# Another conversion of the float64 weights in the first feed-forward layer and in the weight maker, on other steps of the program

## The chip, the cores and the metric

The kernel runs on one core of one Trainium2 chip. The metric is the time of one execution on the device, in microseconds (us). The engines are named as the profile names them: PE (TensorE, matrix products), PEld (its weight loads), DVE (VectorE), ACT (ScalarE), POOL (GpSimd) and SP (SyncE, which here only issues transfers).

## The reference

Three layers follow each other: a causal linear attention with a decaying state per head ("retention"), and two feed-forward layers without a gate. The second and third read float64 weights, the rest is float32.

```python
# 4 batches, 8 heads, 768 positions, 64 wide
state = gamma * state + k[t] outer v[t];  y[t] = scale * q[t] @ state
x = y as (3072 tokens, 512)
h = x @ w_in          # 512 x 2048, float64
x = (h * sigmoid(1.702 * h)) @ w_out     # 2048 x 512, float64
h = x @ moe2_w_in;  r = maximum(h, 0)
out = (r * r) @ moe2_w_out
```

## The kernel before

**Retention.** 24 units of 128 tokens are worked through in the loop of line 553, one step `u` per unit, and one step more. On PE a step is `scores(u)` (L449) and then `outputs(u - 1)`: the products with the masked scores (L498), the update of the state (L508) and the product with the old state (L519). Every sixth unit begins a batch and has no old state, every sixth ends one and has no update. DVE masks the scores (`pt`, L458) and scales the result (L532, L536, L539); ACT scales `v` by head (`vs`, L473; for the first six units POOL does it, L468) and copies the state (L515). A unit is 1 MB, loaded by SP in two halves (L440) into one of four buffers, three steps ahead of its use.

**Slices.** The first feed-forward layer's weights come as 32 slices of 128 x 512 float64 values (512 KB each), in the order of the list `order` (lines 96 to 102): for block `f` of 128 hidden units, slice `(f, 0)` is a part of `w_in` and `(f, 1)` a part of `w_out`. Each is turned into two float32 parts, a high one (the fp32r type that PE reads) and a low one, and PE multiplies low, high and high with (high, high, low) of the activations. `cv_load` issues the load of a slice on POOL's queue into one of three `raw` buffers, at most three slices ahead of the conversions. `cv_a` lets ACT scale the high words into `hm` (L129), at most two ahead. `cv_step` converts: on DVE five instructions on words that take the high part's bits (`top`) and what is left of the mantissa (L158, L156, L166, L173, L177) and one product that gives the low part (L180), on ACT the copy of the high part (L176).

In the retention `cv_step` is called in every step (line 560), and converts on those where its first argument isn't 0 and a scaled slice is there: steps 4, 5, 6, 8, 9, 10 and every second one up to 24, 13 slices in all. The scores' mask and the scaling of the result (`masked`, `scaled`) are put between its instructions.

**First feed-forward layer.** Four blocks `n` of 512 tokens go through 16 steps `f` each (line 707): `up(n, f)` is 12 matmuls with slice `(f, 0)`, and from the third step on `down(n, f - 2)` is 12 matmuls with slice `(f - 2, 1)`. Behind `up`, ACT applies the activation (`gs`, L589, one buffer), rounds it to the high part (`gh`, L590, two buffers), and DVE subtracts it for the low part (`gl`, L594). `down` reads `gh` and `gl`. In block `n = 0` each step also calls `cv_step` (L597), with `gl` put ahead of its last instruction, and a second time at f = 3, 6 and 9: the other 19 slices. In blocks 1 to 3 `background` takes pieces of the generator `make`, up to 4.8 (line 604) of the costs that the pieces give as they yield.

**The maker.** `make` forms, for the second half of the tokens of that layer and for the last layer, sums and differences of weight blocks (seven products in the place of eight), splits them in two parts and writes them to `kw` in DRAM: `make_first` from the slices, `make_second` from 32 more float64 slices that ACT's queue loads (L233), ACT scales (L295) and DVE converts (lines 322 to 340), each written by POOL's queue (L302). What is left by then runs in the stages behind, in portions of 1.8 (lines 815 and 828).

**Last stages.** From line 744 on four blocks of seven-product work run, each an `up2` and a `down2`. Their weights `r` are read from `kw` by SP (L703) as eight buffers come free; all products are of line 756. At its fifth step (`p == 4`) `up2` issues the loads of the next block's activations on POOL's queue (L628, four of 512 KB).

Of the kernel before, what the change touches and what calls it, by code (L numbers as in the profile page):

```python
# [13 lines left out]
U32 = mybir.dt.uint32  # L14
ACTF = mybir.ActivationFunctionType
# [3 lines left out]
P = 128  # L19
# [23 lines left out]
BG = 4.8  # L43
BGUP = 1.8
# [10 lines left out]
def tile_retention_then_two_ffns(  # L55
# [64 lines left out]

    def cv_a():


        n = cv["a"]
        if n == min(cv["load"], cv["b"] + 2):
            return
        cv["a"] += 1
        hm = cv_p.tile([P, 512], F32, tag="hm", name=f"hm{n}")
        nc.scalar.mul(hm, cvt[n][0][:, :, 1].bitcast(F32), 2.0 ** -112)  # L129
        cvt[n].append(hm)  # L130

    def cv_step(limit=len(order), f1=None, f2=None, load=True):

# [4 lines left out]
        if limit is None or n >= min(limit, ready):  # L138
            for f in (f1, f2):
                if f is not None:  # L140
                    f()
        else:
            cv["b"] += 1
            raw, hm = cvt.pop(n)
            hb = hm.bitcast(U32)
            low, high = raw[:, :, 0], raw[:, :, 1]
            f, half = order[n]
            w = wpool[f].tile([P, 4, 2, P], F32R, tag=f"w{half}", name=f"w{n}")
            ws[order[n]] = w
            if cv["pool"] is not None:  # L150
                top, rest = cv["pool"].tile([P, 512], U32, tag="top", name=f"top{n}", bufs=1), high
            else:
                top, rest = high, hb
# [4 lines left out]
            v.tensor_scalar(  # L158
                out=top, in0=hb, scalar1=3, scalar2=0x7FFFF000,
                op0=ALU.logical_shift_left, op1=ALU.bitwise_and,  # L160
            )
            if rest is high:
                do_rest()
            elif f1 is not None:
                f1()
            v.scalar_tensor_tensor(  # L166
                out=top, in0=hb, scalar=0x80000000, in1=top, op0=ALU.bitwise_and, op1=ALU.bitwise_or
            )
            if rest is hb:
                do_rest()  # L170
            elif f1 is not None:
                f1()
            v.scalar_tensor_tensor(  # L173
                out=low.bitcast(F32), in0=low, scalar=2.0 ** -32, in1=rest, op0=ALU.mult, op1=ALU.add
            )
# [4 lines left out]
            v.scalar_tensor_tensor(  # L180
                out=w[:, :, 1], in0=low.bitcast(F32).rearrange("p (k c) -> p k c", c=P), scalar=2.0 ** -20,
                in1=hm.rearrange("p (k c) -> p k c", c=P), op0=ALU.mult, op1=ALU.mult
            )
# [103 lines left out]
    def make_second():  # L287

        with tc.tile_pool(name="k2", bufs=2, side="right", reuse_waits="tile") as pool:
            hms = {}  # L290

            def scale(n):
                if n < len(jobs):
                    hm = pool.tile([P, 512], F32, tag="hm", name=f"hm2_{n}")
                    hms[n] = hm, later(lambda: nc.scalar.mul(hm, raws[n][:, :, 1].bitcast(F32), 2.0 ** -112))  # L295
# [16 lines left out]
            for n in range(len(jobs)):  # L312
                hm, done = hms.pop(n)
                while not done:
# [7 lines left out]
                v.tensor_scalar(  # L322
                    out=wu, in0=hb, scalar1=3, scalar2=0x7FFFFFFF,
                    op0=ALU.logical_shift_left, op1=ALU.bitwise_and,
                )
                yield 0.45
                v.scalar_tensor_tensor(
                    out=wu, in0=hb, scalar=0x80000000, in1=wu, op0=ALU.bitwise_and, op1=ALU.bitwise_or
                )
# [723 lines left out]
```

## Time and profile before

| | us |
|---|---|
| three timed runs | 1069.56, 1072.49, 1075.27 |
| their median | 1072.49 |
| span of the profiled execution | 1070.7 |
| PE busy in it | 1049.9 (98%) |
| DVE busy | 796.5 (74%) |
| ACT busy | 511.6 (48%) |
| POOL busy | 95.0 (9%) |
| mean granted clock of PE | 0.998 of full speed |

The profiled execution is told by its span, from the first to the last instruction; no separate time of it is given, and the span lies 1.8 us under the median of the timed runs. The page cuts the span in 40 slices and gives each engine's busy share in tenths: PE stands at 9 in all but the first two and the last one, while DVE's row moves between 3 and 9. The mean busy share of PE hides where its 20.8 idle us are, so it has to be read by stage. A busy PE is not yet a PE at its peak: matmuls are pipelined, so a step's length is read from the start of one group of matmuls to the start of the next.

### The profile page before, as it was taken

What the parts mean: (1) busy time and instruction counts of PE and PEld (TensorE: products, weight loads), DVE (VectorE), ACT (ScalarE), POOL (GpSimd) and SP (SyncE); (2) the same over time, 40 slices, a digit from 0 to 9 for tenths busy, and PEclk for the clock granted to TensorE, in tenths of its full rate; (3) what the DMA queues carried; (4) which work ended last, traced back from release to release, by engine and by line L of the source; (5) the groups of instructions that cost most, each with busy time, mean ns of one, the idle gap of its engine ahead of it and who ended that gap; (6) DMA issues with size and microseconds to landing.
All of it is one profiled execution on the core that took longest, in us unless ns stands there. A gap on an engine that the chain in (4) does not pass through costs nothing.

```text
span 1070.7 us, 15321 instructions
## 1 busy us (share of the span) xinstructions
PE 1049.9 (98%) x5482; PEld 870.7 (81%) x5482; DVE 796.5 (74%) x1197; ACT 511.6 (48%) x862; POOL 95.0 (9%) x143
## 2 busy tenths in 40 slices
PE   8799999999999999999999999999999999999998
PEld 6788888888888888887888887888888888888886
DVE  4988897888698889855598587889345887345953
ACT  5787554433454545454546343455233465233443
POOL 3100110111111121101000001000100000000000
PEclk9999999999999999999999999999999999999999
DMA  9997677855467685599866799766876667766664
GB/s 331 339 330 275 249 247 255 318 191 191 180 223 248 202 323 189 172 360 317 299 208 204 247 295 326 238 216 210 290 213 193 194 210 230 219 193 192 203 205 163
DMA packets 106652, 259.34 MB, mean 242 GB/s; under 512 B 11216, under 2 KB 11344, under 8 KB 106320
## 3 DMA queue, kind: packets, MB, share of 16 engines
q1 hardware_dynamic: 79088, 156.64, 45.2%
q0 software_dynamic: 22304, 83.89, 21.3%
q10 hardware_dynamic: 5184, 17.83, 5.3%
q8 instruction: 44, 0.72, 0.3%
q14 instruction: 32, 0.26, 0.1%
HBM read 184.91 MB, written 73.40 MB: 241 GB/s over the span
## 4 chain that ended last, share of the span: by engine, by line
PE 89%; DMA 6%; DVE 3%; ACT 1%; SPq 0%; issue 0%; POOL 0%; POOLq 0%; ACTq 0%
PE D L756 28%; PE X L756 15%; PE Z L756 7%; PE y L614 5%; PE h L583 5%; PE h L582 5%; PE y L613 5%; PE y L615 5%; PE h L584 5%; PE Y L756 4%; DMA r<-kw 3%; DMA unit<-qkv 3%; DVE pt L458 1%; PE sc L449 1%; PE yp L519 1%; DMA raw<-w 1%
## 5 line engine op out<-in xcount | busy, mean ns | idle before, releaser
L756 PE MATMUL D<-gx,r 128*128 128x512 f32 x1344 | 306.3, 389 | 0.0
L756 PEld LDWEIGHTS D<-gx,r 128*128 128x128 f32 x1344 | 252.0, 188 | 53.0 <-DVE gx L859 0.8
L859 DVE TENSOR_TENSOR gx<-g,gx 128x1024 fp32r<-128x1024 f32 x112 | 136.3, 1219 | 36.9 <-ACT gx L858 36.7
L858 ACT CAST gx<-g 128x1024 fp32r<-128x1024 f32 x112 | 116.6, 1051 | 93.0 <-PE D L756 83.4
L756 PE MATMUL X<-xh,r 128*128 128x512 f32 x512 | 157.9, 390 | 1.6 <-DMA r<-kw 1.6
L777 ACT COPY g<-X 128x512 f32<-128x512 f32 x96 | 56.4, 588 | 188.5 <-PE X L756 188.5
L782 DVE TENSOR_TENSOR g<-Z,g 128x512 f32<-128x512 f32 x64 | 44.2, 690 | 126.1 <-ACT g L777 93.6
L756 PEld LDWEIGHTS X<-xh,r 128*128 128x128 f32 x512 | 95.9, 188 | 22.6 <-issue 2.8
L582 PE MATMUL h<-hl,w 128*128 128x512 f32 x256 | 99.7, 389 | 0.0
L615 PE MATMUL y<-gl,w 128*128 128x512 f32 x256 | 99.6, 389 | 0.0
L756 PE MATMUL X<-xl,r 128*128 128x512 f32 x256 | 99.6, 389 | 0.0
L584 PE MATMUL h<-hl,w 128*128 128x512 f32 x256 | 99.6, 389 | 0.0
L614 PE MATMUL y<-gh,w 128*128 128x512 f32 x256 | 99.6, 389 | 0.0
L583 PE MATMUL h<-hl,w 128*128 128x512 f32 x256 | 99.6, 389 | 0.0
L613 PE MATMUL y<-gh,w 128*128 128x512 f32 x256 | 99.6, 389 | 0.0
L590 ACT CAST gh<-gs 128x512 fp32r<-128x512 f32 x64 | 39.8, 622 | 87.2 <-PE y L614 84.8
L756 PE MATMUL Z<-xh,r 128*128 128x512 f32 x256 | 79.3, 391 | 1.0 <-DMA r<-kw 0.9
L589 ACT ACTIVATE gs<-h 128x512 f32<-128x512 f32 x64 | 38.2, 597 | 64.5 <-PE h L584 51.6
L594 DVE TENSOR_TENSOR gl<-gs,gh 128x512 fp32r<-128x512 f32 x64 | 44.0, 688 | 32.0 <-ACT gh L590 32.0
L756 PEld LDWEIGHTS Z<-xh,r 128*128 128x128 f32 x256 | 47.7, 188 | 12.3 <-DMA r<-kw 2.3
L613 PEld LDWEIGHTS y<-gh,w 128*128 128x128 f32 x256 | 48.0, 188 | 10.1
L582 PEld LDWEIGHTS h<-hl,w 128*128 128x128 f32 x256 | 48.1, 188 | 10.0
(105 smaller groups left out, 1590.7 us busy)
## 6 DMA issues: line engine op xcount, KB each, us to landing
r<-kw SPq DMA_DIRECT2D x448, 256.0 KB, 2.9
kw<-wq POOLq DMA_DIRECT2D x32, 896.0 KB, 6.5
unit<-qkv SPq DMA_DIRECT2D x47, 512.0 KB, 7.5
raw<-w POOLq DMA_DIRECT2D x32, 512.0 KB, 6.0
kw<-wh POOLq DMA_DIRECT2D x16, 1024.0 KB, 4.7
kw<-w SPq DMA_DIRECT2D x16, 512.0 KB, 4.7
raw<-win ACTq DMA_DIRECT2D x16, 512.0 KB, 4.3
raw<-wout ACTq DMA_DIRECT2D x16, 512.0 KB, 4.7
```

The costliest lines, as they stand in the source:

```text
L582: nc.tensor.matmul(hp, lo[:, k], xh, start=(k == 0), stop=False)
L583: nc.tensor.matmul(hp, hi[:, k], xh, start=False, stop=False)
L584: nc.tensor.matmul(hp, hi[:, k], xl, start=False, stop=(k == KD - 1))
L594: v.tensor_tensor(out=gl, in0=g, in1=gh, op=ALU.subtract)
L613: nc.tensor.matmul(a, lo[:, e], gh, start=s0, stop=False)
L614: nc.tensor.matmul(a, hi[:, e], gh, start=False, stop=False)
L615: nc.tensor.matmul(a, hi[:, e], gl, start=False, stop=s1)
L756: nc.tensor.matmul(a, w, b, start=start, stop=stop, skip_group_check=True)
L777: nc.scalar.copy(out=t, in_=a)
L782: v.tensor_tensor(out=t, in0=a, in1=t, op=ALU.add)
L858: nc.scalar.copy(out=hi, in_=src)
L859: v.tensor_tensor(out=lo, in0=src, in1=hi, op=ALU.subtract)
```

## The change

The conversion of a slice has other instructions, and they stand in other steps.

- `scale_words`: ACT scales the high words into `hm` as before and, new, the low words by 2 to the -29 in place, as integers (3 bits are left of them).
- `join`: two DVE instructions put the 31 bits and the sign together from `hm`, over the high words' place.
- `round_up`: one DVE instruction adds the low word's 3 bits to the lower 16-bit half of the result (every second 16-bit value), with the sum kept from overflowing by a minimum.
- ACT copies the high part from that (L182 now), and the low part is now the difference of the whole and the copy. That instruction (L187) is put in a list, `tails`, and issued in the next `cv_step` behind its first instruction and `f1`. `hm` has three buffers.
- The conversions of the retention are called for on steps 4, 6, ... 22 (`CVU`), and the first loads at step 3. At step 4 no slice is scaled yet, so the conversions stand on steps 6 to 22, nine of them.
- In block `n = 0` each step calls `cv_step` twice until the slices are at an end, 23 of them by f = 11; behind that `background` begins.
- `make_second` uses the same parts: three DVE instructions where there were five, and one ACT instruction more.

```diff
+CVU = range(4, NU, 2)
+    def scale_words(hm, raw):
+        nc.scalar.mul(hm, raw[:, :, 1].bitcast(F32), 2.0 ** -112)
+        nc.scalar.mul(raw[:, :, 0], raw[:, :, 0], 2.0 ** -29)
+    def join(out, hb, other):
+        v.tensor_scalar(
+            out=other, in0=hb, scalar1=3, scalar2=0x7FFFFFFF,
+            op0=ALU.logical_shift_left, op1=ALU.bitwise_and,
+        )
+        yield
+        v.scalar_tensor_tensor(
+            out=out, in0=hb, scalar=0x80000000, in1=other, op0=ALU.bitwise_and, op1=ALU.bitwise_or
+        )
+        yield
+    def round_up(w, raw):
+        half = w.bitcast(U16).rearrange("p (c t) -> p c t", t=2)[:, :, 0]
+        v.scalar_tensor_tensor(out=half, in0=half, scalar=65527.0, in1=raw[:, :, 0], op0=ALU.min, op1=ALU.add)
...
-        hm = cv_p.tile([P, 512], F32, tag="hm", name=f"hm{n}")
-        nc.scalar.mul(hm, cvt[n][0][:, :, 1].bitcast(F32), 2.0 ** -112)
+        hm = cv_p.tile([P, 512], F32, tag="hm", name=f"hm{n}", bufs=3)
+        scale_words(hm, cvt[n][0])
...
-            def do_rest():
-                v.tensor_scalar(out=rest, in0=hb, scalar1=0x1FF, scalar2=None, op0=ALU.bitwise_and)
...
-            v.scalar_tensor_tensor(
-                out=low.bitcast(F32), in0=low, scalar=2.0 ** -32, in1=rest, op0=ALU.mult, op1=ALU.add
-            )
-            nc.scalar.copy(out=w[:, :, 0], in_=top.bitcast(F32).rearrange("p (k c) -> p k c", c=P))
-            v.tensor_scalar(out=hb, in0=top, scalar1=0xFF800000, scalar2=None, op0=ALU.bitwise_and)
+            steps = join(hm.bitcast(U32), hm.bitcast(U32), raw[:, :, 1])
+            next(steps)
+            if f1 is not None:
                 f1()
+            cv_tail()
+            next(steps)
+            round_up(hm, raw)
+            nc.scalar.copy(out=w[:, :, 0], in_=hm.rearrange("p (k c) -> p k c", c=P))
             if f2 is not None:
                 f2()
...
+            def tail():
+                v.tensor_tensor(
+                    out=w[:, :, 1], in0=hm.rearrange("p (k c) -> p k c", c=P), in1=w[:, :, 0], op=ALU.subtract
+                )
+                ws[key] = w
+            tails.append(tail)
...
-                v.tensor_scalar(out=hb, in0=wu, scalar1=0xFF800000, scalar2=None, op0=ALU.bitwise_and)
-                yield 0.45
-                v.scalar_tensor_tensor(
-                    out=hm, in0=raw[:, :, 0], scalar=2.0 ** -52, in1=hm, op0=ALU.mult, op1=ALU.mult
-                )
+                round_up(wf, raw)
...
-                v.tensor_tensor(out=wf, in0=wf, in1=hm, op=ALU.add)
-                yield 0.7
...
-                cv_step(2 * WA if u >= 3 and (u % 2 != 1 or u in (3, 5, 9)) else 0, masked, scaled, u >= 2)
+                cv_step(2 * WA if u in CVU else 0, masked, scaled, u >= 3)
...
-            if n == 0:
+            if n == 0 and cv["b"] < len(order):
                 cv_step(len(order), None, low)
-                if f in (3, 6, 9):
-                    cv_step()
+                cv_step()
```

Three places show it in the engines' order. The first is DVE in two steps of the retention's middle, before: every step's mask (`pt`) stands among a slice's six instructions.

```order
L158 TENSOR_SCALAR top_685<-hm_571 128x512
L156 TENSOR_SCALAR raw_476<-hm_571 128x512
L166 SCALAR_TENSOR_TENSOR top_685<-hm_571,top_685 128x512
L458 TENSOR_TENSOR pt_647<-sc_638,tab_sb 128x1024
L173 SCALAR_TENSOR_TENSOR raw_476<-raw_476 128x512
L177 TENSOR_SCALAR hm_571<-top_685 128x512
L532 TENSOR_TENSOR x_0_680<-yp_657,ytab_136 128x2x128
L532 TENSOR_TENSOR x_1_681<-yp_657,ytab_136 128x2x128
L180 SCALAR_TENSOR_TENSOR w_684<-raw_476,hm_571 128x4x128
L158 TENSOR_SCALAR top_746<-hm_682 128x512
```

And now, in the same engine and stage:

```order
L130 TENSOR_SCALAR raw_338<-hm_450 128x512
L461 TENSOR_TENSOR pt_562<-sc_553,tab_sb 128x1024
L135 SCALAR_TENSOR_TENSOR hm_450<-hm_450,raw_338 128x512
L143 SCALAR_TENSOR_TENSOR hm_450<-hm_450,raw_338 128x512
L535 TENSOR_TENSOR x_0_444<-yp_572,ytab_135 128x2x128
L535 TENSOR_TENSOR x_1_445<-yp_572,ytab_135 128x2x128
L461 TENSOR_TENSOR pt_617<-sc_608,tab_sb 128x1024
L535 TENSOR_TENSOR x_0_650<-yp_627,ytab_136 128x2x128
L535 TENSOR_TENSOR x_1_651<-yp_627,ytab_136 128x2x128
L187 TENSOR_TENSOR w_595<-hm_450,w_595 128x4x128
```

One instruction of a slice stands ahead of the mask in the place of three, the next step has none but the tail, and a slice takes two steps.

The second place is DVE at f = 1 of the first feed-forward layer's block 0, before: one slice.

```order
L158 TENSOR_SCALAR raw_1378<-hm_1492 128x512
L166 SCALAR_TENSOR_TENSOR raw_1378<-hm_1492,raw_1378 128x512
L156 TENSOR_SCALAR hm_1492<-hm_1492 128x512
L173 SCALAR_TENSOR_TENSOR raw_1378<-raw_1378,hm_1492 128x512
L177 TENSOR_SCALAR hm_1492<-raw_1378 128x512
L594 TENSOR_TENSOR gl_1_1511<-gs_1_1509,gh_1_1510 128x512
L180 SCALAR_TENSOR_TENSOR w_1514<-raw_1378,hm_1492 128x4x128
```

Now the same step on DVE, from its first slice to the next step's `gl`:

```order
L130 TENSOR_SCALAR raw_1321<-hm_1423 128x512
L187 TENSOR_TENSOR w_1428<-hm_1365,w_1428 128x4x128
L135 SCALAR_TENSOR_TENSOR hm_1423<-hm_1423,raw_1321 128x512
L143 SCALAR_TENSOR_TENSOR hm_1423<-hm_1423,raw_1321 128x512
L597 TENSOR_TENSOR gl_1_1454<-gs_1_1452,gh_1_1453 128x512
L130 TENSOR_SCALAR raw_1426<-hm_1434 128x512
L187 TENSOR_TENSOR w_1457<-hm_1423,w_1457 128x4x128
L135 SCALAR_TENSOR_TENSOR hm_1434<-hm_1434,raw_1426 128x512
L143 SCALAR_TENSOR_TENSOR hm_1434<-hm_1434,raw_1426 128x512
```

And on ACT there, where the second slice's copy and the scaling of the slice after next now stand between one `gh` and the next `gs`:

```order
L592 ACTIVATE gs_1_1452<-h_1_1439 128x512
L593 CAST gh_1_1453<-gs_1_1452 128x512
L182 CAST w_1457<-hm_1423 128x4x128
L125 ACTIVATE hm_1464<-raw_1437 128x512
L126 ACTIVATE raw_1437<-raw_1437 128x512
L182 CAST w_1469<-hm_1434 128x4x128
L125 ACTIVATE hm_1475<-raw_1467 128x512
L126 ACTIVATE raw_1467<-raw_1467 128x512
L592 ACTIVATE gs_2_1495<-h_2_1480 128x512
```

Where one slice's copy and one scaling stood between two activations there are now six instructions, and each tail (L187) reads what ACT has copied just before.

The third place is POOL's queue around the first `up2`'s loads of activations (`xb`), before: three of the maker's writes (`kw`) stand between the end of the first layer (`ykept_122`) and those loads, and more behind them.

```order
L623 DMA ykept_122<-y_1_4445 128x1024
L302 DMA kw_112<-wq_4374 128x7x256
L302 DMA kw_112<-wq_4599 128x7x256
L302 DMA kw_113<-wq_4726 128x7x256
L628 DMA xb_0_0_0_4810<-ykept_119 128x1024
L628 DMA xb_0_0_1_4811<-ykept_119 128x1024
L628 DMA xb_0_1_0_4814<-ykept_120 128x1024
L628 DMA xb_0_1_1_4815<-ykept_120 128x1024
L302 DMA kw_113<-wq_4851 128x7x256
L302 DMA kw_114<-wq_4979 128x7x256
```

Now the last of the maker's writes (`kw_116`) stands ahead of them:

```order
L625 DMA ykept_122<-y_1_4485 128x1024
L314 DMA kw_115<-wq_4409 128x7x256
L314 DMA kw_115<-wq_4565 128x7x256
L314 DMA kw_116<-wq_4688 128x7x256
L314 DMA kw_116<-wq_4769 128x7x256
L630 DMA xb_0_0_0_4844<-ykept_119 128x1024
L630 DMA xb_0_0_1_4845<-ykept_119 128x1024
```

The maker is at an end seven of its writes earlier, counted against the loads.

## Rows read from the trace of the kernel before

**Rows 1.** Busy us by stretch: stretch, length, busy (instructions) of each engine, clock, DMA share, GB/s.

```profile
0.00:104.00 104.00, 89.79 (x1257) 78.60 (x1258) 82.68 (x151) 77.30 (x248) 15.79 (x28) 0.98 0.91 328
104.00:453.00 349.00, 349.00 (x1543) 288.98 (x1542) 301.57 (x556) 166.34 (x255) 49.40 (x68) 1.00 0.65 228
453.00:528.00 75.00, 73.19 (x321) 59.47 (x320) 41.65 (x72) 37.91 (x65) 7.78 (x10) 1.00 0.92 328
607.00:683.00 76.00, 75.28 (x331) 61.74 (x330) 56.48 (x96) 29.92 (x48) 7.98 (x11) 1.00 0.89 296
```

**Rows 2.** PE by time, retention: start us, us, engine, line, operation [idle before].

```profile
38.31 1.16 PE L449 MATMUL sc<-unit 64*128 64x128 f32 x16
...
63.58 1.16 PE L449 MATMUL sc<-unit 64*128 64x128 f32 x16 [2.10 <-DMA unit<-qkv]
...
72.49 1.16 PE L449 MATMUL sc<-unit 64*128 64x128 f32 x16
...
76.16 1.16 PE L449 MATMUL sc<-unit 64*128 64x128 f32 x16
...
98.38 1.16 PE L449 MATMUL sc<-unit 64*128 64x128 f32 x16 [0.26 <-DMA unit<-qkv]
...
104.12 0.48 PE L582 MATMUL h<-hl,w 128*128 128x512 f32 x1
```

**Rows 3.** Waits of PE, 0 to 110 us: total, times, longest.

```profile
PE sc L449 <- DMA unit<-qkv: 5.7, 6, 2.1
PE yp L498 <- DVE pt L458: 4.2, 4, 2.5
```

**Rows 4.** DVE by time in one step of the retention.

```profile
45.20 0.41 DVE L158 TENSOR_SCALAR top<-hm 128x512 uint32<-128x512 uint32 x1
45.54 0.42 DVE L156 TENSOR_SCALAR raw<-hm 128x512 uint32<-128x512 uint32 x1
...
49.81 0.41 DVE L158 TENSOR_SCALAR top<-hm 128x512 uint32<-128x512 uint32 x1
```

**Rows 5.** Busy us by stretch, one microsecond of the retention (columns as in rows 1).

```profile
65.00:66.00 1.00, 1.00 (x12) 1.00 (x10) 1.00 (x2) 1.00 (x5) 0.00 (x0) 0.50 1.02 422
```

**Rows 6.** ACT by time, block 0 of the first feed-forward layer.

```profile
120.59 0.62 ACT L590 CAST gh<-gs 128x512 fp32r<-128x512 f32 x1 [1.95 <-PE y L614]
...
123.63 0.66 ACT L176 CAST w<-raw 128x512 fp32r<-128x512 f32 x1 [1.29 <-DVE raw L166]
124.20 0.68 ACT L129 ACTIVATE hm<-raw 128x512 f32<-128x512 f32 x1
124.78 0.58 ACT L589 ACTIVATE gs<-h 128x512 f32<-128x512 f32 x1
```

**Rows 7.** DVE by time in the same microseconds.

```profile
121.24 0.69 DVE L594 TENSOR_TENSOR gl<-gs,gh 128x512 fp32r<-128x512 f32 x1 [0.50 <-ACT gh L590]
...
122.45 0.42 DVE L158 TENSOR_SCALAR raw<-hm 128x512 uint32<-128x512 uint32 x1
122.91 0.69 DVE L166 SCALAR_TENSOR_TENSOR raw<-hm,raw 128x512 uint32<-128x512 uint32 x1
123.64 0.43 DVE L156 TENSOR_SCALAR hm<-hm 128x512 uint32<-128x512 uint32 x1
```

**Rows 8.** Slices' loads in all, 104 to 215 us, from the view by tile.

```profile
DMA to landing us min/median/max: 3.4/5.3/8.3
```

**Rows 9.** DMA issues, 120 to 140 us: queue, count, KB each, median us to landing.

```profile
raw<-w POOLq DMA_DIRECT2D x5, 512.0 KB, 7.1
```

**Rows 10.** DMA issues, 160 to 180 us.

```profile
raw<-w POOLq DMA_DIRECT2D x3, 512.0 KB, 3.8
```

**Rows 11.** Waits of PE, 480 to 512 us (first `up2`).

```profile
PE X L756 <- DMA r<-kw: 1.1, 2, 0.6
```

**Rows 12.** POOL's queue by time around it.

```profile
490.96 0.93 POOL L302 DMA_DIRECT2D kw<-wq  x1 [14.86 <-ACT g L784]
491.88 2.29 POOL L628 DMA_DIRECT2D xb<-ykept  x4
```

More of the change, by code (lines that the diff above doesn't have):

```diff
@@ L127, in cv_a, with cv_tail @@
         cv["a"] += 1
-        hm = cv_p.tile([P, 512], F32, tag="hm", name=f"hm{n}")
-        nc.scalar.mul(hm, cvt[n][0][:, :, 1].bitcast(F32), 2.0 ** -112)
+        hm = cv_p.tile([P, 512], F32, tag="hm", name=f"hm{n}", bufs=3)
+        scale_words(hm, cvt[n][0])
         cvt[n].append(hm)
+    tails = deque()
+    def cv_tail():
+        while tails:
+            tails.popleft()()
     def cv_step(limit=len(order), f1=None, f2=None, load=True):
@@ L138, in cv_step @@
         if limit is None or n >= min(limit, ready):
-            for f in (f1, f2):
+            for f in (f1, f2, cv_tail):
                 if f is not None:
@@ L144, in cv_step @@
             raw, hm = cvt.pop(n)
[L145 to L153, printed above, removed]
-            def do_rest():
-                v.tensor_scalar(out=rest, in0=hb, scalar1=0x1FF, scalar2=None, op0=ALU.bitwise_and)
@@ L158, in cv_step @@
-            v.tensor_scalar(
-                out=top, in0=hb, scalar1=3, scalar2=0x7FFFF000,
-                op0=ALU.logical_shift_left, op1=ALU.bitwise_and,
-            )
-            if rest is high:
-                do_rest()
-            elif f1 is not None:
-                f1()
-            v.scalar_tensor_tensor(
-                out=top, in0=hb, scalar=0x80000000, in1=top, op0=ALU.bitwise_and, op1=ALU.bitwise_or
-            )
[L169 to L172, printed above, removed]
@@ L173, in cv_step @@
-            v.scalar_tensor_tensor(
-                out=low.bitcast(F32), in0=low, scalar=2.0 ** -32, in1=rest, op0=ALU.mult, op1=ALU.add
-            )
-            nc.scalar.copy(out=w[:, :, 0], in_=top.bitcast(F32).rearrange("p (k c) -> p k c", c=P))
-            v.tensor_scalar(out=hb, in0=top, scalar1=0xFF800000, scalar2=None, op0=ALU.bitwise_and)
+            key = order[n]
+            w = wpool[key[0]].tile([P, 4, 2, P], F32R, tag=f"w{key[1]}", name=f"w{n}")
+            steps = join(hm.bitcast(U32), hm.bitcast(U32), raw[:, :, 1])
@@ L193, in weights @@
         while (f, s) not in ws:
-            cv_step()
+            if tails:
+                cv_tail()
+            else:
+                cv_step()
         return ws[f, s][:, :, 0], ws[f, s][:, :, 1]
@@ L294, in scale @@
                     hm = pool.tile([P, 512], F32, tag="hm", name=f"hm2_{n}")
-                    hms[n] = hm, later(lambda: nc.scalar.mul(hm, raws[n][:, :, 1].bitcast(F32), 2.0 ** -112))
+                    hms[n] = hm, later(lambda: scale_words(hm, raws[n]))
             def low(n, w, t, done):
@@ L321, in make_second @@
                 wu = wf.bitcast(U32)
[L322 to L325, printed above, removed]
+                steps = join(wu, hb, wu)
+                next(steps)
                 yield 0.45
-                v.scalar_tensor_tensor(
-                    out=wu, in0=hb, scalar=0x80000000, in1=wu, op0=ALU.bitwise_and, op1=ALU.bitwise_or
-                )
+                next(steps)
                 yield 0.7
-                v.tensor_scalar(out=hb, in0=wu, scalar1=0xFF800000, scalar2=None, op0=ALU.bitwise_and)
-                yield 0.45
-                v.scalar_tensor_tensor(
-                    out=hm, in0=raw[:, :, 0], scalar=2.0 ** -52, in1=hm, op0=ALU.mult, op1=ALU.mult
-                )
+                round_up(wf, raw)
                 later(lambda n=n: load(n + 2))
@@ L356, in make @@
             cv_step()
+        cv_tail()
         cv_ctx.close()
```

7 lines of the change are left out of this document (2 added, 5 removed).

## The prediction

> **What bounds the kernel now.** I read the busy times by stretch first. From 104 to 453 us, the four blocks of the first feed-forward layer, PE is busy 349.0 of 349.0 us, while DVE has 301.6 and ACT 166.3 [rows 1]: there only PE sets the pace, and whatever other engines save is worth nothing, but what they lose can cost. The 64 steps of that stretch take 349 / 64 = 5.45 us each. Where PE is idle is worth something: 104.0 - 89.8 = 14.2 us in the retention, 1.8 and 0.7 in the first two `up2` (453 to 528, 607 to 683) [rows 1].
>
> Then the retention by time. Fifteen steps lie between the scores at 38.31 and at 98.38, 60.07 us or 4.00 each; a step in which PE waits for nothing takes 76.16 - 72.49 = 3.67 [rows 2]. PE's waits there are for the unit's load (5.7 us in all) and for DVE's mask (4.2, the longest 2.5) [rows 3]. So the stage is held in turn by DVE, by the transfers and by PE, and the change touches the first two.
>
> **The change in the retention.** DVE goes from one slice's first instruction to the next one's in 49.81 - 45.20 = 4.61 us [rows 4], over a PE step: in these stretches DVE sets the step. Now a slice has four instructions in the place of six and takes two steps; by the order one of them stands ahead of the mask. Of the 4.61, the old slice has three of 0.34 and three of 0.60 [rows 4, 7], 2.8; the 1.8 of mask and scaling stay, half of 0.34 + 3 x 0.60 comes on top, and DVE's mean step is 2.9. Next in line are the transfers and PE. How fast those two are together the trace shows, since from 63.58 to 98.38 the kernel before already converts on every second step only: nine steps in 34.80 us [rows 2]. In it lies a stretch with the granted clock at 0.50, PE's lower level of 1.2 GHz, behind a PE wait of 2.10 [rows 5, 2]; the two steps from 63.58 to 72.49 took 8.91 where 2 x 3.67 = 7.34 would do, so the clock cost 1.57. Without it a step is (34.80 - 1.57) / 9 = 3.69. Fifteen of them are 55.4 in the place of 60.1: -4.7. The mask's longest wait, 2.5, lies ahead of 38.31 and goes too. Together **-7.2 us**. By bytes it fits: twelve slices are loaded by the end of the retention in the place of fifteen, 1.6 MB less, and at the 328 GB/s of the stretch [rows 1] that is 4.8 us. ACT has nine slices with three instructions, 27, for 13 with two, 26: no more than before. What could hide the gain is ACT's first scaling, which waits for a load issued later than before with the casts of the first block's activations behind it. Ends: steps stay at 34.80 / 9 = 3.87 and one microsecond goes at the start, -3.5; all of PE's idle time but the first 2 us goes, -12.
>
> **The change in block 0.** Nineteen slices with PE never waiting become 23 in twelve steps, two per step. In the order a loop closes over ACT and DVE: `gh`, `gl`, the second slice's first join, the first slice's tail, second join, rounding, the copy on ACT, two scalings, the next `gs`, the next `gh`. From start to start: `gh` to `gl` 121.24 - 120.59 = 0.65 [rows 6, 7]; `gl` and the tail 0.60 each, as two instructions fill 121.24 to 122.45 [rows 7]; the first join with an unrelated instruction behind it 0.34 [rows 4]; the second join with the rounding waiting for it 123.64 - 122.91 = 0.73 [rows 7]; rounding to copy as 122.91 to 123.63, 0.72 [rows 7, 6]; copy to scaling 0.57, scaling to the next 0.58 twice, `gs` to `gh` 0.60 [rows 6]. The sum is 0.65 + 0.60 + 0.34 + 0.60 + 0.73 + 0.72 + 0.57 + 0.58 + 0.58 + 0.60 = 5.97 us per step, 0.5 over PE's 5.45.
>
> Two of these have no row. The scaling of integers in place is taken as the scaling of the high words (0.58); from 0.3 to 1.2 it would move the loop by -0.3 to +0.6 a step. The rounding on 16-bit halves is taken as a DVE instruction of two inputs (0.69); 0.35 to 1.2 moves it by -0.3 to +0.5. Both come once in the loop. I keep the nearest rows.
>
> The second loop is the loads'. Three `raw` buffers mean that slice n + 3 is loaded when slice n is rounded. From landing to rounding is, for a step's first slice, two scalings 1.16, the copy before it 0.71, the tail 0.60 and the second join 0.73, 3.2; for its second slice `gs` and `gh` stand between, 4.3. The rounding's end and the issue behind it take about 1.05. Six slices, three steps, then need 2 L + 3.2 + 4.3 + 2.1 = 2 L + 9.6, where L is the time from issue to landing. In this stage L was 3.4 to 8.3, median 5.3 [rows 8]: 7.1 while the writes of `xkept` and `kw` ran [rows 9], 3.8 with few transfers beside [rows 10]. With 5.3 a step takes (10.6 + 9.6) / 3 = 6.73; with 3.8, 5.73, and then the first loop's 5.97 holds.
>
> How long PE forgives this: PE does `up` alone in the first two steps (2.73 each), so `down(f)` starts 8.2 + 5.45 f after the layer's start and reads `gl` 0.46 later; `gl` is there 0.65 + 0.69 behind the start of `gh`. So `gh(f)` may start as late as 7.3 + 5.45 f. It first starts at 2.73 + 0.15 + 0.6 = 3.5. Two slices a step end at f = 11, where the limit is 67.3. Three steps at 5.97 (nothing else is in transfer yet) and eight at 6.73 bring it to 3.5 + 17.9 + 53.8 = 75.2. PE waits the difference: **+7.9 us**. Ends: 5.97 throughout, 69.2, +1.9; L = 7.1 to the end, 7.93 a step, 84.8, +17.5. Behind f = 11 nothing is late any more. The weights themselves are not what is missed: `up(f)` needs slice 2 f - 1, and 9 + 2 f are converted by then.
>
> The Trainium skill (DMA: Bandwidth & Descriptors, "Anatomy of one DMA — SWDGE (gpsimd) path") fits such a transfer as 2.0 us and bytes over 436 GB/s, an estimate of 3.2 us for a slice. The trace has 3.4 only as its minimum [rows 8]; by the page's figure the load's loop would never hold and the wait would be the 1.9 of the first rival.
>
> **The change in the maker.** `make_second` loses two DVE instructions per slice and gains one on ACT, 32 x 0.58 = 19 us on an engine that is busy 166 of 349; PE covers both [rows 1]. But it starts in block 0 and gives less cost per slice, so its last write stands ahead of the first `up2`'s activation loads. Before, a write of 896 KB went out at 490.96 with four loads right behind it [rows 12], and PE then waited for weights [rows 11]; the second `up2` repeats it. Of the idle 1.8 + 0.7 [rows 1] I leave 0.2 for the loads alone: **-2.3 us**. Ends: 0 and -2.5.
>
> **Sum.** The profiled execution's span is 1070.7, 1.8 under the median of the timed runs, 1072.5; the terms are differences, so I put them on the median: 1072.5 - 7.2 + 7.9 - 2.3 = 1070.9.
>
> **The rivals.**
> - *Loads land fast.* Nothing but slices and part of `kw` is in transfer, L stays under 4.2, where the second loop equals the first, and the wait is 1.9: 1072.5 - 7.2 + 1.9 - 2.3 = 1064.9. For it speaks the 3.8 [rows 10], against it that 1 MB of slices and 0.75 MB of `kw` now share a step of 6 us.
> - *Loads land late* (slower). Slices, `kw` and `xkept` come in fewer microseconds, and the 7.1 of rows 9 lasts through the block: wait 17.5, 1080.5. It is slower by 0.5% from a wait of 14.9, a step of 7.6, L = 6.6.
> - *The waits bring the clock down.* PE waits 1 to 3 us at most steps from f = 6 on. The 2.10 wait of rows 2 was followed by a clock of 0.50 [rows 5], at a price of 1.57. Four such falls give 1077.2. Against it: the waits are between 5 us of matmuls. The Trainium skill (TensorE: Matmul & The Clock Gate, "HAM oscillation — how this bites in real kernels") describes a loop whose every round waits and starts throttled; the rows show one such fall and no loop of them.
> - *The retention gains little.* The unit's loads, issued only when PE gives a buffer back, set the step, as in the 5.7 us of rows 3: -3.5 in the place of -7.2, 1074.6.
>
> That the change doesn't do what it says holds in one point that is certain: nine slices, not ten, are converted in the retention; the sums count nine.
>
> **How the numbers follow.** The forecast 0.46, its own range 1066 to 1076 (wait 3 to 13); fast loads 0.26; late loads 0.12; clock 0.09; little gain 0.07. A measurement of this kernel tells about 0.5%, 5.4 us, from no change: under 1067.1 or over 1077.9. Faster is the first rival and a little of the forecast, 0.28; slower the second, half of the third and a little of the forecast, 0.18; the rest, 0.54, is within. The range runs from fast loads with a larger gain in the retention, 1063, to late loads, 1081.
>
> **What would show it.** The first `h` of the layer at about 97, not 104.1, with steps of about 3.7 and no wait for the mask. PE waits of line 615 to 617 for `gl` or `gh` from about f = 6 to 11, some 8 us, gone in block 1. Slice loads of 5 us there, `gh` to `gh` 6 to 7. No wait for `r` at the first two activation loads. It is wrong if PE shows no wait in block 0 (a loop summed too long), or if the first `h` comes after 101.

## The result, and the profile after

The changed kernel takes 1079.33 us (median of 4 runs, 1077.13 to 1080.78); the kernel before, beside it, 1072.57. The ratio is 1.0068 with a 95% interval of 1.0044 to 1.0091: slower, by 0.44 to 0.91%. The forecast was 1070.9, a gain of 1.6; the time lies inside the range of 1063 to 1081, but on the other side of no change, where 0.18 of the chance had been put. The profiled execution took 1078.58, its span is 1076.8 where that of before was 1070.7: +6.1 to explain.

Four points cut both spans into the pieces of the forecast. First the kernel before, ACT's first `gh` of block 0 and of block 1 (L590) and PE's first `X` (its first `h` was at 104.12):

```profile
107.84 0.62 ACT L590 CAST gh<-gs 128x512 fp32r<-128x512 f32 x1
...
192.11 0.62 ACT L590 CAST gh<-gs 128x512 fp32r<-128x512 f32 x1
...
452.45 0.62 PE L756 MATMUL X<-xh,r 128*128 128x512 f32 x2
```

The same points of the changed kernel, with its first `h`:

```profile
95.55 0.48 PE L585 MATMUL h<-hl,w 128*128 128x512 f32 x1
...
99.23 0.62 ACT L593 CAST gh<-gs 128x512 fp32r<-128x512 f32 x1
...
198.21 0.62 ACT L593 CAST gh<-gs 128x512 fp32r<-128x512 f32 x1
...
460.25 0.62 PE L758 MATMUL X<-xh,r 128*128 128x512 f32 x2
```

| piece | forecast | from the rows | measured |
|---|---|---|---|
| retention, to the first `h` | -7.2 | 95.55 - 104.12 | -8.6 |
| block 0, `gh` to `gh` of block 1 | +7.9 | 98.98 - 84.27 | +14.7 |
| blocks 1 to 3, from there to the first `X` | 0 | 262.04 - 260.34 | +1.7 |
| from the first `X` to the end | -2.3 | 616.55 - 618.25 | -1.7 |
| sum | -1.6 | | +6.1 |

One term carries the error: block 0 costs 14.7 and not 7.9. PE's waits, in the form of [rows 3] (total, times, longest; whole span):

```profile
PE y L615 <- ACT gh L593: 8.3, 5, 2.9
PE sc L452 <- DMA unit<-qkv: 4.7, 7, 1.4
...
PE h L587 <- DVE hl L400: 0.9, 1, 0.9
PE y L617 <- DVE gl L597: 0.6, 1, 0.6
```

The mask's row of [rows 3] is gone, and the wait for `gh` is there with 8.3, close to the forecast. The busy times by stretch agree with it: from 95.4 to 180 PE has 76.3 of 84.6 us, 8.3 idle, where the kernel before had no idle time [rows 1]. But both show less than was lost, since a group that runs slowly counts as busy: a group of twelve `y` matmuls took 3.3 in the place of 2.9 five times, when its third one also waited for `gl`, and 4.76 once, at a lower clock. The columns are those of [rows 1].

```profile
0.00:95.40 95.40, 87.14 (x1256) 76.17 (x1257) 68.25 (x112) 79.43 (x253) 14.02 (x25) 1.00 0.93 341
95.40:180.00 84.60, 76.29 (x317) 59.00 (x316) 64.20 (x108) 53.56 (x93) 11.70 (x22) 0.98 0.72 244
180.00:460.10 280.10, 278.56 (x1225) 229.07 (x1224) 229.31 (x428) 152.42 (x232) 43.93 (x55) 1.00 0.70 247
```

Both loops of the forecast can be read off. A step in which no load has to be waited for, from ACT's rows, takes 105.24 - 99.23 = 6.01; the sum of ten terms had given 5.97. The integer scaling in place (L126) takes one pitch of 0.57, the rounding on 16-bit halves 0.76 (assumed: 0.58 and 0.69):

```profile
99.76 0.62 ACT L182 CAST w<-hm 128x512 fp32r<-128x512 f32 x1
...
103.48 0.66 ACT L125 ACTIVATE hm<-raw 128x512 f32<-128x512 f32 x1
104.05 0.68 ACT L126 ACTIVATE raw<-raw 128x512 uint32<-128x512 uint32 x1
104.61 0.59 ACT L592 ACTIVATE gs<-h 128x512 f32<-128x512 f32 x1
105.24 0.62 ACT L593 CAST gh<-gs 128x512 fp32r<-128x512 f32 x1
```

The slowest step takes 127.98 - 118.17 = 9.81. ACT sits in front of the scaling of a slice whose load was issued at 118.98, 2.3 us behind a 1 MB write of `xkept`, and landed 7.3 us later; `gs` and `gh`, for which PE waits, are queued behind it (ACT, then POOL):

```profile
118.17 0.62 ACT L593 CAST gh<-gs 128x512 fp32r<-128x512 f32 x1
...
120.94 0.70 ACT L125 ACTIVATE hm<-raw 128x512 f32<-128x512 f32 x1 [1.62 <-DMA raw<-w]
...
126.26 0.66 ACT L125 ACTIVATE hm<-raw 128x512 f32<-128x512 f32 x1 [3.54 <-DMA raw<-w]
...
127.98 0.62 ACT L593 CAST gh<-gs 128x512 fp32r<-128x512 f32 x1
```

```profile
116.71 0.54 POOL L721 DMA_DIRECT2D xkept<-xout  x1
118.98 0.53 POOL L120 DMA_DIRECT2D raw<-w  x1 [1.73 <-ACT gh L593]
122.40 0.53 POOL L120 DMA_DIRECT2D raw<-w  x1 [2.89 <-ACT raw L126]
122.92 0.54 POOL L721 DMA_DIRECT2D xkept<-xout  x1
```

At the border of blocks 0 and 1 stands a wait that was not in the forecast. The last `gl` of block 0 and the four `hl` of block 1 stand on DVE behind the maker's pieces (L278 to L292), which now start in block 0 (DVE, then PE):

```profile
192.94 0.43 DVE L286 TENSOR_TENSOR wt<-wf 128x256 f32<-128x256 f32 x1
193.28 0.42 DVE L287 TENSOR_TENSOR wt<-wf 128x256 f32<-128x256 f32 x1
193.62 0.68 DVE L597 TENSOR_TENSOR gl<-gs,gh 128x512 fp32r<-128x512 f32 x1
194.22 2.49 DVE L400 TENSOR_TENSOR hl<-x,hl 128x512 fp32r<-128x512 f32 x4
```

```profile
194.96 0.50 PE L587 MATMUL h<-hl,w 128*128 128x512 f32 x1 [0.88 <-DVE hl L400]
```

### The profile page after: what moved, and what is told of

The parts are those of the page before. It is cut to its first block, busy times and chain, and to the rows that moved or that the text cites. A ratio compares the mean times of both kernels' runs of the same rounds, so it can differ in the third digit from the quotient of the medians.

```text
span 1076.8 us, 15237 instructions
## 1 busy us (share of the span) xinstructions
PE 1053.5 (98%) x5482; PEld 867.9 (81%) x5482; DVE 743.7 (69%) x1069; ACT 547.0 (51%) x926; POOL 93.9 (9%) x143
## 4 chain that ended last, share of the span: by engine, by line
PE 73%; DMA 12%; DVE 7%; ACT 4%; issue 2%; POOL 0%; SPq 0%; DVEq 0%; ACTq 0%; POOLq 0%
PE D L758 28%; PE X L758 15%; PE Z L758 8%; DMA unit<-qkv 4%; PE Y L758 4%; DMA raw<-w 3%; PE h L587 3%; PE h L585 3%; PE h L586 3%; PE y L617 3%; PE y L615 3%; PE y L616 3%; DMA r<-kw 2%; DMA raw<-wout 1%; ACT vs L476 1%
## 5 line engine op out<-in xcount | busy, mean ns | idle before, releaser
L758 PEld LDWEIGHTS X<-xh,r 128*128 128x128 f32 x512 | 95.6, 188 | 22.4 <-issue 1.4
L617 PEld LDWEIGHTS y<-gl,w 128*128 128x128 f32 x256 | 48.4, 189 | 14.5 <-DVE gl L597 4.8
L125 ACT ACTIVATE hm<-raw 128x512 f32<-128x512 f32 x64 | 43.2, 674 | 28.4 <-DMA raw<-w 18.4
```

The source lines that it names most:

```text
L617: nc.tensor.matmul(a, hi[:, e], gl, start=False, stop=s1)
L758: nc.tensor.matmul(a, w, b, start=start, stop=stop, skip_group_check=True)
```

## The experiments

The theory: the loss in block 0 comes from two slices per step, converted in line with `gh` and `gl`, at the pace of the loop over three `raw` buffers (6.9 us a step) with the loop of ACT and DVE (6.0) under it. Rivals: the new instructions cost wherever they stand; the clock; the maker; the transfers as such. All edits are against the changed kernel, but for the fourth. The time is the median of a kernel's runs; the ratio is to the kernel before as timed beside them. "PE's loss" is `gh` to `gh` of block 1 minus the 84.27 of the kernel before.

| kernel | first `h` | gh(0) to gh(11) | PE's loss | time | ratio to before |
|---|---|---|---|---|---|
| before | 104.1 | 56.3 | 0 | 1072.6 | |
| changed | 95.6 | 76.0 | 14.7 | 1079.3 | 1.0068 (1.0044 to 1.0091) |
| e1 old places | 102.3 | 56.3 | 0 (4.4 in block 1) | 1075.3 | 1.0031 (1.0018 to 1.0044) |
| e2 four `raw` | 99.1 | 66.7 | 5.4 | 1071.6 | 0.9998 (0.9987 to 1.0010) |
| e3 maker later | 95.9 | 76.8 | 14.3 | 1079.9 | 1.0078 (1.0057 to 1.0099) |
| e4 maker alone | 107.2 | 56.3 | 0 | 1075.6 | 1.0024 (1.0001 to 1.0047) |
| e5 paced | 98.3 | 61.9 | 9.4 | 1076.9 | 1.0056 (1.0039 to 1.0073) |
| e6 four, paced | 99.5 | 60.6 | 0.6 | 1066.3 | 0.9947 (0.9930 to 0.9963) |
| e7 old places, tail | 102.6 | 56.3 | 0 | 1071.9 | 0.9998 (0.9985 to 1.0010) |
| e8 no low scaling | 96.7 | 73.2 | 11.9 | 1075.1 (one run) | |
| e9 `xkept` later | 99.1 | 74.6 | 13.3 | 1078.7 | 1.0075 (1.0050 to 1.0101) |
| e10 `kw` later | 96.9 | 72.5 | 11.2 | 1076.1 | 1.0041 (1.0021 to 1.0061) |
| e11 both later | 94.8 | 70.0 | 8.7 | 1071.5 | 0.9999 (0.9983 to 1.0015) |

**e1: the new conversion in the old places.**

```diff
-                cv_step(2 * WA if u in CVU else 0, masked, scaled, u >= 3)
+                cv_step(2 * WA if u >= 3 and (u % 2 != 1 or u in (3, 5, 9)) else 0, masked, scaled, u >= 2)
...
-            if n == 0 and cv["b"] < len(order):
+            if n == 0:
                 cv_step(len(order), None, low)
-                cv_step()
+                if f in (3, 6, 9):
+                    cv_step()
```

> The changed kernel with its new conversion everywhere, but the slices placed as before: 13 in the retention (five steps in a row from step 3), then one per step of block 0 and three extra ones at f = 3, 6, 9. Theory (the loss lies in two slices per step of block 0): PE waits for nothing from the first h to the end of block 0, so the +14.7 us of the first layer's block 0 are gone; the retention keeps part of its gain, since a new slice with mask and scaling takes DVE some 4.0 us where the old one took 4.61: first h at about 100, time 1066 to 1069. Rival (the new instructions are what costs, wherever they stand): PE still waits over 5 us in block 0, time over 1074. Second rival (transfers set the retention, 13 slices instead of 9 bring the old length back): first h at 103 to 104.5, no waits in block 0, time 1071 to 1073.

Through block 0 PE waits for nothing, so the first rival falls: the placement costs, not the instructions. The time was still 6 us over the theory. The first `h` came at 102.25, two microseconds later than the theory's 100 and just under the second rival's 103 to 104.5 (e7, with the same places, has 102.60), so most of the retention's gain needs the smaller number of slices there. And there was a wait that no expectation had named: PE for the low half of the last weights, at the start of block 1, followed by a stretch at a lower clock (PE by time; then two stretches by busy time, clock in the third column from the end):

```profile
192.23 0.58 PE L616 MATMUL y<-gh,w 128*128 128x512 f32 x1 [2.67 <-DVE w L187]
```

```profile
192.00:194.00 2.00, 1.77 (x5) 1.40 (x6) 1.97 (x5) 0.00 (x0) 0.00 (x0) 0.63 0.98 261
194.00:196.00 2.00, 2.00 (x7) 1.55 (x6) 1.93 (x5) 0.59 (x1) 0.00 (x0) 0.52 1.06 301
```

**e2: four `raw` buffers.**

```diff
-        if n >= cv["b"] + 3:
+        if n >= cv["b"] + 4:
...
-        hm = cv_p.tile([P, 512], F32, tag="hm", name=f"hm{n}", bufs=3)
-        scale_words(hm, cvt[n][0])
-        cvt[n].append(hm)
+        raw = cvt[n][0]
+        scale_words(raw[:, :, 1].bitcast(F32), raw)
...
```

(`raw` gets 4 buffers; `hm`, 2 buffers, is first written by the join.)

> The changed kernel with four raw buffers in the place of three, so that slice n + 4 is loaded when slice n is rounded; to make room the high words are scaled in place and two hm buffers do. Theory (the loop over three raw buffers and the load sets the 6.9 us per step): the load loop falls to about (5.9 + 4.8) / 4 x 2 = 5.4 us a step, the ACT and DVE loop of 6.0 is left, gh(11) comes some 70 us after the layer's start where it came at 79.7, PE's loss in block 0 falls from 14.7 to 3 to 5 us and the time to 1068 to 1071. Rival (ACT and DVE's own work and the clock fall make the step, loads are only what happens to end last): gh to gh stays at 6.7 to 7.0 and the time at 1077 to 1081. Against both: one slice more is loaded in the retention, 0 to +1.6 us there.

The theory held: the time is 7.8 us lower, and `gh` follows `gh` in the 6.0 to 6.1 of the ACT and DVE loop at seven of the eleven steps. One of them, ACT by time:

```profile
158.59 0.62 ACT L593 CAST gh<-gs 128x512 fp32r<-128x512 f32 x1
...
164.66 0.62 ACT L593 CAST gh<-gs 128x512 fp32r<-128x512 f32 x1
```

PE's waits for `gh` fall from 8.3 to 1.0. The loads landed no sooner than in the changed kernel (median 5.1, the longest 8.3); what the fourth buffer takes away is the wait for them. Without the border's 1.2 the loss is 5.4 - 1.2, so the work of ACT and DVE alone had cost some 4 us of the 14.7; the rest hung on the loop over the buffers.

**e3: the maker starts with block 1.**

```diff
-                if f < NF - 1:
+                if n > 0 and f < NF - 1:
                     background(BG if n < NSTD - 1 or f < 5 else BG - 1.6)
```

> The changed kernel, but the maker of the second layer's operands starts with block 1 and has no turn in the last steps of block 0. Theory (the maker's pieces on DVE in front of gl and hl cost PE 1.2 us at the border of blocks 0 and 1): that wait is gone, the rest of block 0's loss (13.4 us) stays, and the gain in the up2 stages (1.7 us) is partly given back: 1077.5 to 1079.5. Rival (the earlier maker and its kw writes slow the slice loads of block 0 and make most of the loss): gh to gh falls towards 6.2 and the time to 1072 or less.

No wait for `hl` is left, the loss inside block 0 is as large as before, and what lies behind the first `X` takes 1077.9 - 459.66 = 618.2 again, not 616.6. The maker is not what makes block 0 slow; its earlier start buys 1.7 at the end and costs 1.2 at the border.

**e4: only `make_second` in its new form, in the kernel before.** (Its edit is the diff's part on `make_second`, with `scale_words`, `join` and `round_up`.)

> The kernel before with only the second layer's maker in its new form (two DVE instructions less and one ACT instruction more per slice). Theory (the new maker takes PE's waits for r in the up2 stages and costs nothing in the blocks): 1070.0 to 1072.5, PE's r waits fall from 2.5 to about 1, retention and block 0 as before. Rival (the extra ACT instruction and the changed order of activation loads cost PE in block 3, where the changed kernel loses 1.7 us): PE waits for gl or gh in block 3 of 1 to 2 us, 1072.5 to 1074.

Neither: from the first `X` to the end it takes 1074.2 - 455.84 = 618.4, with 2.5 us of waits for `r`, as before. The cheaper maker by itself gains nothing; the gain of the changed kernel comes from the earlier start. Nearly the whole difference of the two spans, 3.0 of 3.5, lies where nothing was changed: up to the second layer's maker this kernel has the instructions of the kernel before in their order, and its first `h` came 3 us later.

```profile
107.16 0.47 PE L595 MATMUL h<-hl,w 128*128 128x512 f32 x1
```

PE's waits for the loads of `unit` are 7.5 us here and were 5.7 [rows 3]; why they land later, no run shows. So the retention's length differs between profiles of the same instructions: among the six kernels with the changed kernel's retention (changed, e3, e5, e9, e10, e11) the first `h` stands at 94.8 to 99.1.

**e5: slices paced over fourteen steps.**

```diff
+ONE = (1, 3, 5, 7, 10)
...
                 cv_step(len(order), None, low)
-                cv_step()
+                if f not in ONE:
+                    cv_step()
```

> The changed kernel with one edit: the 23 slices of block 0 are spread over fourteen steps (one slice instead of two at f = 1, 3, 5, 7, 10), still with three raw buffers. Theory (a slice takes 3.45 us in the loop of loads, two of them before the next gh are 6.9 a step against PE's 5.45; with 1.6 per step gh(10) comes behind 16 slices at about 59 us where PE asks for it at 61.8, and no weight is late): the +13.4 us of PE's loss inside block 0 fall to 0 to 3, the 1.2 at the border of block 1 may stay: 1065 to 1069, PE waits for gh under 2 us. Rival (the sum of work on DVE and ACT, the clock or the shared transfers slow block 0, however the slices are spread): PE waits for gh stay above 5 us and the time above 1074.

Half right. Up to f = 11 PE waits for nothing, as worked out (gh(10) at 158.92 - 98.33 = 60.6 behind the first `h`, against 61.8). Then the bill comes: a late `gh` stops PE at 180, the group behind it takes 4.64 at a lower clock (0.56 from 182 to 184), the last slices are done at 182 to 186, the maker's pieces follow, and `hl` of block 1 is later than in the changed kernel; that `h` group takes 6.89 in the place of 2.88 (PE's waits).

```profile
PE h L588 <- DVE hl L401: 3.7, 1, 3.7
PE y L617 <- ACT gh L594: 2.0, 2, 1.8
```

Pacing moves the lateness to the end of the block; it does not take it away while each of the 23 slices needs the loop's 3.4 to 3.5 us.

**e6: four buffers, paced, less of the maker in block 0.** The edit of e2 with the fourth buffer used from block 0 on, and:

```diff
+ONE = (3, 6, 9)
...
-                cv_step()
+                if f not in ONE:
+                    cv_step()
...
-                    background(BG if n < NSTD - 1 or f < 5 else BG - 1.6)
+                    background(BG if 0 < n < NSTD - 1 or n > 0 and f < 5 else BG - 1.6)
```

> Four raw buffers from block 0 on (three in the retention), one slice instead of two at f = 3, 6, 9, and 1.6 us less of the maker per step in the last steps of block 0. Theory (with four buffers the ACT and DVE loop of 6.0 us a step is left, 0.55 over PE's step, and three single steps win back over 1 us each; less of the maker lets hl of block 1 come in time): no PE wait in block 0 and at its border, retention as in the changed kernel (first h at 95.5 to 97): 1063 to 1067. Rival (what is left in the four-buffer run, five groups stretched by 0.4 us and 1.2 at the border, does not come from the loop): 1068 to 1071.

As the theory said, but for the first `h`, which came at 99.5 and not at 95.5 to 97. It is the best version: 1066.31, faster than the kernel before by 0.37 to 0.70%. PE is busy through the whole block, and 0.2 is left of the wait at the border (stretch with busy times, then the wait):

```profile
99.40:180.00 80.60, 80.60 (x359) 66.76 (x358) 66.88 (x114) 54.85 (x97) 11.13 (x21) 1.00 0.76 264
```

```profile
PE h L588 <- DVE hl L401: 0.2, 1, 0.2
```

**e7: e1 with the last subtraction in its own step.**

```diff
                 if f in (3, 6, 9):
                     cv_step()
+                if f == NF - 1:
+                    cv_tail()
```

> The kernel of the run with the old places, with one edit: the subtraction that ends the last slice is issued in its own step and not behind block 1's activations. Theory (PE's single wait of 2.7 us for w at the start of block 1 and the clock fall behind it, together 4.4 us, come from that deferred subtraction alone): 1070 to 1072, no PE wait in block 0 or 1, first h at about 102. Rival (the wait moves to gl or hl, since DVE has the same work there): 1073 to 1076.

The wait of e1 and its slow stretch are gone, and nothing takes their place. With the new instructions in the old places the kernel is as fast as before, no more: what the cheaper conversion is worth comes from placing it elsewhere.

**e8: no scaling of the low words.**

```diff
-        scale_words(hm, cvt[n][0])
+        nc.scalar.mul(hm, cvt[n][0][:, :, 1].bitcast(F32), 2.0 ** -112)
```

> The changed kernel without the in-place integer scaling of the low words on ACT in the first layer's conversion (so the rounding there adds an unscaled word; the values are not the reference's). Theory (the scaling of 0.58 stands once per slice in both loops): the unhindered step falls from 6.0 to 5.4, the step in the load loop from 7.1 to 6.5, gh(11) comes 4 to 6 us earlier and PE's loss in block 0 falls from 14.7 to 8 to 11, time 1072 to 1076. Rival (ACT is no part of the loops, as it idles 18 us there waiting for loads): gh to gh stays within 0.15 and the time at 1077 to 1081.

The unhindered step falls by one instruction, 105.80 - 100.37 = 5.43, so ACT is in that loop. gh(11) comes only 2.8 earlier, though, under the 4 to 6 expected. In this profile the last fourteen slices' loads took 5.6 in the mean, where those of the changed kernel took 5.3, so they may have taken part of the gain back.

**e9 and e10: which transfers make the loads late.** e9 issues `xkept`'s writes at f = 10 and 11; e10 puts the four `kw` writes of `make_first` in POOL's queue:

```diff
-                if n == 0 and f in (2, 3):
-                    j = XHELD + f - 2
+                if n == 0 and f in (10, 11):
+                    j = XHELD + f - 10
```

> The changed kernel with one edit: the two 1 MB writes of xkept are issued at f = 10 and 11 of block 0 and not at f = 2 and 3. In the changed kernel two of the slice loads right behind them took 7.2 us from issue to landing, the median of the block being 4.7. Theory (in the loop over three raw buffers a load that lands late is paid almost whole): the 9.8 us step at f = 3 to 4 falls to 6 to 7, gh(11) comes 3 to 5 us earlier than the 76.0 us behind gh(0) of the changed kernel, time 1074.5 to 1077. Rival (the 7.2 us come from the slices and kw themselves, or the late load is absorbed by the buffers): gh(11) stays within 1.5 us of 76.0, time 1078 to 1081.

```diff
-                        nc.sync.dma_start(out=dst[:, A11:A12 + 1], in_=f0)
+                        nc.gpsimd.dma_start(out=dst[:, A11:A12 + 1], in_=f0)
...
```

> The changed kernel with one edit: the first layer's kw writes (0.75 MB a step, which SP issues in block 0 as soon as a pair of slices is converted) stand in POOL's queue behind the last slice load, so that they go out after block 0's conversion. Theory (the slice loads share the transfers with these writes, as they did not with xkept's): loads land in about 4 us, none above 5.5 but those behind xkept, the step falls from 6.9 to 6.1 to 6.4, gh(11) comes 66 to 70 us behind gh(0) where it came at 76.0, time 1071 to 1075. Rival (the loads of slices are late by themselves, by their own burst of two and their release): loads keep a median of 4.7 and a longest of 6.5 to 7.5, gh(11) stays at 74 to 77, time 1077 to 1081.

e9 came out as its rival had it: the slow step did not go, it came later (ACT by time, 137.32 - 128.32 = 9.0, with loads of up to 6.7 beside the `kw` writes), one of 9.55 stood at f = 8, and gh(11) gained 1.4. e10 lay between both expectations: the median of a load fell from 4.7 to 4.0 (view by tile), ten of the eleven steps took 6.3 on average, as expected, but the one behind `xkept` still took 9.6. The slow step of e9:

```profile
128.32 0.62 ACT L593 CAST gh<-gs 128x512 fp32r<-128x512 f32 x1
...
130.44 0.69 ACT L125 ACTIVATE hm<-raw 128x512 f32<-128x512 f32 x1 [0.98 <-DMA raw<-w]
...
135.61 0.66 ACT L125 ACTIVATE hm<-raw 128x512 f32<-128x512 f32 x1 [2.95 <-DMA raw<-w]
...
137.32 0.62 ACT L593 CAST gh<-gs 128x512 fp32r<-128x512 f32 x1
```

**e11: both writes later**, with three buffers and two slices per step as in the changed kernel.

> The changed kernel with both edits of the last two runs: xkept's writes at f = 10 and 11, the first layer's kw writes behind the last slice load. With kw later alone, ten of the eleven steps took 6.3 us on average and one, behind an xkept write, 9.6. Theory (each of the two kinds of writes makes slice loads late, and each alone leaves the other): no step over 7.2, gh(11) 66.5 to 69.5 us behind gh(0), PE's loss in block 0 with its border 5 to 8 us where it was 14.7, time 1070 to 1074. Rival (one load in the block lands late whatever else is in transfer): one step of 9 us stays, gh(11) at 72 or more, time 1075 to 1079.

Near the theory (gh(11) at 70.0 where 69.5 was its end, a loss of 8.7 where 8 was): no step over 7.5 (7.2 expected), and the time of the kernel before. So what the two kinds of writes add to the loads is worth 14.7 - 8.7 = 6 us of the loss; the rest is the loop with loads of 4.0, its own length, and the border. Loads in the view by tile, of e10 and of e11 (it also holds two loads of the next layer's weights; the longest of e11's slices took 5.2):

```profile
DMA to landing us min/median/max: 3.4/4.0/6.8
```

```profile
DMA to landing us min/median/max: 3.4/4.0/6.0
```

## Why the prediction was wrong, step by step

- **The retention** was right in mechanism and a little small: -8.6 for -7.2, the mask's wait gone, the clock at 1.00. One profile of it is good to some 2 us either way (e4), so the difference says nothing: the first `h` at 95.6 is near the early end of the 94.8 to 99.1, whose mean, 96.8, is nearer to the forecast's 97. The rival of a little gain, -3.5, is met by none of the six.
- **Block 0 is the step that failed**: the mechanism was right (PE waits for `gh`, from f = 4 on, gone in block 1, two slices per step as its cause: e1, e2, e6), its size was half of the truth. By the working of the forecast `gh(11)` was to start 75.2 behind the first `h`; it started 175.24 - 95.55 = 79.7, with the limit at 67.3 a wait of 12.4 for 7.9. Of the 4.5 the eight steps taken at 6.73 make 3.2 (175.24 - 118.17 = 57.07 for 53.8), the three taken at 5.97 1.0 (they took 18.94), the first `gh` 0.2.

  The term mis-sized is the 9.6 in the load's loop, 2 L + 9.6 for three steps (3.2 + 4.3 + 2 x 1.05): what passes between the landing of a slice and the issue that its rounding releases. The L of 5.3 was right: the fourteen loads behind those eight steps, issued from 118.98 on, took 7.2, 5.1, 7.2, 5.3, 5.2, 5.3, 4.1, 4.0, 4.7, 7.4, 5.8, 4.1, 4.2 and 4.4, in the mean 5.3.

  But from landing to rounding a step's second slice took 4.6 to 4.7 wherever ACT had waited for it, not 4.3: on DVE `gl` and the slice's own first join stand ahead of the tail, and the forecast's path went past them. A first slice took 3.1 to 4.4, 3.7 in the mean of nine, not 3.2, as it comes behind the rounding of the slice before. From the start of a rounding to the issue it took 1.30 and not 1.05. Together 3.7 + 4.7 + 2 x 1.3 = 11.0, and (2 x 5.3 + 11.0) / 3 = 7.2 is what the eight steps took, 57.07 / 8 = 7.1.

  The slice that landed at 126.26 (ACT's row above), on DVE and then its issue on POOL, 130.89 - 126.26 = 4.63 and 132.19 - 130.89 = 1.30:

```profile
128.63 0.69 DVE L597 TENSOR_TENSOR gl<-gs,gh 128x512 fp32r<-128x512 f32 x1 [3.71 <-ACT gh L593]
129.24 0.42 DVE L130 TENSOR_SCALAR raw<-hm 128x512 uint32<-128x512 uint32 x1
129.57 0.68 DVE L187 TENSOR_TENSOR w<-hm,w 128x512 fp32r<-128x512 f32 x1
130.18 0.68 DVE L135 SCALAR_TENSOR_TENSOR hm<-hm,raw 128x512 uint32<-128x512 uint32 x1
130.89 0.75 DVE L143 SCALAR_TENSOR_TENSOR hm<-hm,raw 128x512 uint16<-128x512 uint16 x1
...
132.19 0.53 POOL L120 DMA_DIRECT2D raw<-w  x1 [6.20 <-DVE raw L130]
```

  e11 bears it out: its loads of 4.0 with the forecast's 9.6 would leave steps of 5.97, and with 11.0 they give 6.3; its eight steps took (70.0 - 18.85) / 8 = 6.4, where 18.85 is its first three. What slower loads cost was sized right: 7.9 - 1.9 = 6.0 in the forecast, 6 from e11 to the changed kernel. No run changed the order on DVE by itself, so that share is read from the rows and not tested.
- **Two waits were left out.** `gl(11)` came 176.72 - 175.24 = 1.5 behind its `gh` and not 0.65, since the second slice's rounding stood ahead of it on DVE, 0.8 more; and the border cost 1.2. With 12.4 this makes 14.4 of the 14.7.
- **The late-loads rival** (17.5 of wait, 1080.5) is the case that came nearest in time, with 0.12, and in part by luck. The writes of `kw` and `xkept` together do make loads late (e9 to e11), but the rival had them at 7.1 throughout and a step of 7.9, where three took 7.2 to 7.4, the mean was 5.3 and the eight steps took 7.1. At f = 11 the wait was 12.4; the two other waits and the 1.7 of blocks 1 to 3, which it did not have, brought the time near.
- **Fast loads** had 0.26 and did not come, but its price was wrong as well: in e11 its condition holds (median 4.0, under its 4.2), and the loss is 8.7 where it had 1.9, by the same 11.0 and the same two waits. The Trainium skill's figure (DMA: Bandwidth & Descriptors, "Anatomy of one DMA — SWDGE (gpsimd) path"), an estimate of 3.2, is not reached by any slice of these runs; the shortest took 3.3, in e2.
- **The clock** was no cause. PE fell to its lower level once, behind a wait of 2.89 (128 to 133 us, clock 0.50), and that `y` group took 4.76 in the place of 2.88; but PE had to wait for `gh` again from 142.99 on, up to f = 10, so the 1.9 us came out of these later waits. No loop of such falls is there, as against "HAM oscillation — how this bites in real kernels" (TensorE: Matmul & The Clock Gate, the Trainium skill). Stretches of the changed kernel:

```profile
126.00:128.60 2.60, 0.00 (x0) 0.00 (x0) 0.00 (x0) 2.31 (x5) 0.00 (x0) 1.00 1.01 419
128.60:130.00 1.40, 1.35 (x4) 0.83 (x5) 1.37 (x3) 1.40 (x3) 0.00 (x0) 0.69 1.00 391
130.00:132.00 2.00, 2.00 (x6) 1.61 (x5) 1.92 (x4) 0.59 (x2) 0.00 (x0) 0.50 1.02 395
```

- **The maker**: -1.7 for -2.3, but by the earlier start alone (e3, e4), not by the cheaper slice.
- **Blocks 1 to 3** had been given 0 and cost 1.7, in block 3: ACT waits up to 3.5 there for the loads of the next stage's operands with `gs` behind, and the last `gl` waits on DVE behind those operands (0.6). e2, e6 and e9 don't have it; what decides it was not tried.

## What to carry to other kernels

Work that is moved under a stage where one engine is the bound is free only if the loop it brings, through every engine and buffer it passes, is shorter than that engine's step. Work each loop out along the order of instructions on every engine: what stands ahead of an instruction in its queue belongs to the loop, and here 1.4 us in three steps were left out so. Where such a loop is too long, look for what makes it wait before moving the work back: here a fourth buffer, a slice less at three steps and a little less of the work behind it turned 0.7% slower into 0.5% faster. Pacing alone only moves the lateness to the next thing in line.

## What was not expected of the hardware

- A 512 KB slice landed in 4.0 us in the median without the `kw` writes (e10) and in 4.5 with them (the changed kernel's twenty), but the two issued 2.3 and 2.6 us behind a 1 MB write took 7.2; one beside `kw` writes alone took 7.4.
- The retention, with the same instructions in the same order, ended 3 us apart in two profiles (104.12 and 107.16), and between 94.8 and 99.1 in six.
- The two operations without a row were as cheap as their nearest ones: ACT's integer scaling in place 0.67 with a pitch of 0.57, DVE's 16-bit minimum and addition at stride two 0.76 for 512 elements against 0.69 at 32 bits.
